# Attention with relative bias, then a maxout feed-forward: the order of VectorE's work in batch one's second pass, and of batch four's DMA transposes

## The chip, the cores and the metric

The kernel runs on one core of a Trainium2 chip. A core has five engines, each with its own instruction stream: TensorE (PE, with its weight loads listed apart as PEld), VectorE (DVE), ScalarE (ACT), GpSimd (POOL) and SyncE (SP). They run side by side and meet at semaphores. DMAs are issued by an engine's stream and carried out by 16 DMA engines. The metric is the time of one execution on the device, in microseconds (us), less is better.

## The reference

Attention over 8 batches and 8 heads of 576 tokens with 64 numbers each, with a bias that depends on the distance of two tokens only; its output, turned to one row of 512 per token, goes through a feed-forward with three gates of which the largest is kept.

```python
scores = scale * np.matmul(q, k.transpose(0, 1, 3, 2))
bias = bias_table[bucket]                       # bucket of |i - j|
scores = scores + bias.transpose(2, 0, 1)[None, :, :, :]
attn = np.exp(scores - max); attn = attn / (sum + 1e-09)
x = np.matmul(attn, v)                          # to (4608, 512)
h = np.maximum(np.maximum(x @ w1, x @ w2), x @ w3)
return (h @ w_out)
```

## The kernel before

**Tiling.** The heads are worked on in pairs (`hp` 0 to 3), the tokens in four tiles of 128 and a rest of 64. `b` counts the batches from 0: batch one is `b = 0`, batch four is `b = 3`. Queries and keys stand turned, with the head's numbers along the partitions, in `qT` and `kT` (two buffers each, one for every other batch).

**A pair's work.** `visit` makes the scores of one half of the queries on TensorE (tiles `sc`) and their exponentials on ScalarE (into `e4`). The rest of 64 keys goes through `left_keys` (scores `sct`), the rest of 64 queries through `left_queries` (scores `scq`), both into `el`. The bias is a factor after the exponential. It differs from a constant only near the diagonal, so VectorE multiplies bands alone: `times_band` takes one key tile's band in `e4` with `hank`, a table of the factors in SBUF; `times_bandt` and `times_band_left` (together `products`) do the same for `el`, the first with `bandt`, a mirrored copy of a part of `hank` that `make_bandt` makes once with two copies. `attend` then makes the weighted sums of one half (`half` 0 or 1) in PSUM tile `a` and returns `quotients`, the division on VectorE (a reciprocal, L730, and a multiplication, L731, into `x_sb`).

**Batch one** is done in two passes, since its data come in late. The first pass makes the scores of the first half of the queries for all four pairs; each pair's `attend` of half 0 is put on the list `late`. The second pass makes the second half and takes one or two entries from `late` for every pair (`next_late`). In pair 0 and 1 it runs two of them, with `bands(2)` and `bands(3)`, the first pass's bands of pairs 2 and 3, between them. `late_bands` are the three bands of the second pass of the pair itself. In the midst of each pair's `visit`, `more_transposes(hp + 1)` turns the next pair's remaining queries on TensorE, and a VectorE copy (L110, `qT<-tp`, 128x320) brings them to `qT`. `x_transposes` turns the finished output into `xT` on TensorE, and ScalarE copies it. Here and later `fill` puts in portions of the feed-forward.

**Order.** Matmuls, VectorE's and ScalarE's operations run in the order of the program (`inorder`); exponentials are free in this stage. So what stands ahead of an operation in the program on the same engine must be over before it starts.

**Batches two to eight.** Batch two's queries and keys are turned on TensorE. From batch three on, `transposes(b)` lets SP issue DMA transposes from `q_sb`, `k_sb` and the tails into `qT` and `kT`: it is a generator, and every `next(crossbar)` issues the q and the k transpose of one tile (`t` 0 to 3, then the tail as `t` 4), L550. SP also issues the stores of finished output rows (`store_outputs`, which issues what has been put on `stores`) and the transposes of `x_sb` into `xT` (L741). In the loop over `b` and `hp` there are two places for `next(crossbar)` per pair: behind the first `visit`, and behind the second half of the scores. For `b` 2 the first place issues in pairs 1 to 3, the second in pairs 1 and 2, each behind a call of `store_outputs`.

**Loads tied to transposes.** GpSimd's queue issues the loads of q, k and v. `go_behind` makes a load wait for a transpose: `load_v(b + 1)` in pair 2 of `b` 2 waits for `turned_qk[3, 1, 2]`, the key transpose of tile 2 of batch four, and `load_qk(b + 2)`, the loads of batch five, for that of tile 3. TensorE needs tile 2 and 3 of the keys in the second `scores` of pair 0, and the tail of the keys in `left_keys`.

Of the kernel before, what the change touches and what calls it, by code (L numbers as in the profile page):

```python
# [39 lines left out]
def kernel(  # L40
# [68 lines left out]
    def dve_copy(out_, in_):  # L109
        return inorder(nc.vector.tensor_copy(out_, in_))  # L110
# [199 lines left out]
    def make_bandt():  # L310
        for par in range(2):
            r = slice(64 * par, 64 * par + 64)
            c = BAND // 2 - 64 * par
            dve_copy(bandt[r, :, :], hank[r, par::2, c : c + 192][:, :, ::-1])
# [337 lines left out]
    def visit(qT, kT, e4, c, mid=None, el=None):  # L652

        if el is not None:
            banks = [ps_a.tile([P, KT * 64], F32, tag="a", name="scq") for _ in range(2)]
            turn_left_queries(qT, kT, banks)
            put_left_queries(el, banks)
        for tt in range(0, KT, 2):
            scores(qT, kT, e4, c, tt)
            if tt == 0 and mid:  # L660
                mid()
# [12 lines left out]
    def times_bandt(hp, el):  # L674
        return inorder(nc.vector.tensor_tensor(
            out=el[:, S - 192 : S], in0=el[:, S - 192 : S], in1=bandt[:, hp, :], op=ALU.mult
        ))
# [8 lines left out]
    def times_band_left(hp, el):  # L686
        last_tile = el[:, S + P * KT - P :].rearrange("p (h q) -> p h q", h=2)
        inorder(nc.vector.tensor_tensor(
            out=last_tile, in0=last_tile, in1=hank[:, 2 * hp : 2 * hp + 2, P - 64 : P][:, :, ::-1], op=ALU.mult,
        ))  # L690
# [69 lines left out]
    def next_late():  # L760
        return late.pop(0)() if late else (lambda: None)

    def e_tiles():
        return (
            ep.tile([P, KT, 2, QM], BF16, tag="e4", name="e4"),
            ep.tile([P, S + KT * P], BF16, tag="el", name="el"),
        )
# [37 lines left out]
    def bands(hp):  # L805
        for t in range(KT):
            times_band(hp, first_e[hp], t, 0, QS, inorder)
# [9 lines left out]
    for hp in range(HP):  # L817
        qT, kT = (x[:, hp, :] for x in qk[0])
        e4, el = e_tiles()
# [22 lines left out]
    def products(hp, el):  # L842
        times_bandt(hp, el)
        times_band_left(hp, el)

    for hp in range(HP):
        qT, kT = (x[:, hp, :] for x in qk[0])
        e4, el = e_tiles()  # L850
        visit(qT, kT, e4, 1, (lambda: more_transposes(hp + 1)) if hp + 1 < HP else None)

        def keys():
            left_keys(hp, qT, kT, el, QS, S)

        def queries():
            left_queries(hp, qT, kT, el)

        def late_bands():
            for t in range(KT):  # L860
                times_band(hp, e4, t, QS, QM, inorder)

        if hp == 0:
            keys()
        if hp == 1:
            x_transposes(0, 0)
        quotients = next_late()
        if hp < 2:
            quotients()
            if hp == 0:  # L870
                bands(2)
            else:
                keys()
            queries()
            if hp == 1:
                x_transposes(1, 0)
            quotients = next_late()
            quotients()
            if hp == 0:
                bands(3)  # L880
                make_bandt()
            late_bands()
            products(hp, el)
        else:
            keys()
            quotients()
            queries()
            late_bands()
            if hp == 2:
                x_transposes(2, 0)  # L890
                x_transposes(3, 0)
                add_ffn(0, QS)
                fill(8)
            else:
                batch[2] = load_tiles()
                load_qk(2)
                x_transposes(0, 1)
                fill(8, lambda: second_transposes(qk[1], 0))
            products(hp, el)
        late.append(lambda hp=hp, e4=e4, el=el: attend(0, hp, e4, el, 1))  # L900

    turned = [lambda hp=hp: x_transposes(hp, 1) for hp in range(1, HP)]
    for b, hp in [(b, hp) for b in range(1, B) for hp in range(HP)]:
        if hp == 0:
            x_sb[b] = x_tile()
        qT, kT = (x[:, hp, :] for x in qk[b])
        e4, el = e_tiles()
        together = b > 1 and (b, hp) != (2, 0)
        tiled = bool(stages)
        rate = 8 if b == 1 or (b, hp) == (2, 0) else 13  # L910

        visit(qT, kT, e4, 0)
        store_outputs()
        if b == 1:
            if hp == 0:
                crossbar = transposes(2)
            next(crossbar, None)
        elif hp and b + 1 < B:  # L920
            if hp == 1:
                crossbar = transposes(b + 1)
            next(crossbar)
        early()
        if turned:
            turned.pop(0)()
        quotients = next_late()
        if not tiled:
            times_band(hp, e4, 0, 0, QS, inorder)
        quotients()  # L930
        if b == 1 and hp + 1 < HP:
            spread_packed(hp + 1, nc.vector)
        if (b, hp) == (1, 1):
            add_ffn(QS, QS)

        def keys():
            sums_first = together and (not tiled or len(pending) < 2)
            if sums_first:
                next_late()()
            left_keys(hp, qT, kT, el, 0, S)  # L940
            if together and not sums_first:
                next_late()()

        if tiled:
            if len(pending) > 1:
                fill(DCH)
            keys()
            fill(FCH)
            times_band(hp, e4, 0, 0, QS, inorder)
            begin0, end0, begin1, end1, after = stages.pop(0)  # L950
            scores(qT, kT, e4, 1, 0)
            begin0()
            exp_left = left_queries(hp, qT, kT, el)
            turned_1 = begin1()
            times_band(hp, e4, 1, 0, QM, inorder)
            band_left = times_bandt(hp, el)
            go_behind([band_left], turned_1[-1])
            times_band_left(hp, el)
            scores(qT, kT, e4, 1, 2)
            dve0 = end0([exp_left])  # L960
            dve1 = end1([band_left])
            times_band(hp, e4, 2, 0, QM, inorder)
            dve0()
            times_band(hp, e4, 3, 0, QM, inorder)
            dve1()
            pending.extend((n, [fn]) for n, fn in after)
        else:
            fill(8 if (b, hp) == (2, 1) else rate, keys, *([lambda: None] if together else []))
            times_bandt(hp, el)
            visit(qT, kT, e4, 1, el=el if together else None)  # L970
        store_outputs()
        if b == 1 or hp in (1, 2) and b + 1 < B:
            next(crossbar, None)
        early()
        if turned:
            turned.pop(0)()
        if not together:
            quotients = next_late()
            times_band(hp, e4, 1, 0, QM, inorder)
            quotients()  # L980
        if b == 1 and hp + 1 < HP:
            second_transposes(qk[1], hp + 1)
        if hp == 1 and b > 1:
            pending.extend((n, [fn]) for n, fn in rest)
            rest.clear()
            made, tail = ffn((b - 1) * CH, CH, False, True)
        if hp == (2, 2, 0)[min(b, 3) - 1] and b + 1 < B:
            load_v(b + 1, 0, H, turned_qk[b + 1, 1, b] if b < 3 else None)
            if b == 1:
                load_last_weights(turned_qk[2, 1, KT - 1])  # L990
                batch[3] = load_tiles()
                load_qk(3, turned_qk[2, 1, KT - 1])
        if hp == 2 and 1 < b < B - 2:
            batch[b + 2] = load_tiles()
            load_qk(b + 2, turned_qk[b + 1, 1, KT - 1])

        def queries():
            if not together:
                left_queries(hp, qT, kT, el)
            times_band(hp, e4, 3, 0, QM, inorder)  # L1000

        def bands_2():
            for t in range(1 if together else 2, 3):
                times_band(hp, e4, t, 0, QM, inorder)

        if not tiled:
            fill(rate, bands_2, queries)
            times_band_left(hp, el)
        if hp == 1 and b > 1:
            stages.extend(made)  # L1010
            strict.append(b)
        for half in range(2):
            late.append(lambda b=b, hp=hp, e4=e4, el=el, half=half: attend(b, hp, e4, el, half))
# [48 lines left out]
```

## Time and profile before

The median of 5 runs is 315.74 us (315.17 to 316.11).

| What | us |
|---|---|
| profiled execution | 315.74 |
| its span | 314.0 |
| PE busy | 300.7 |
| ACT busy | 205.2 |
| DVE busy | 213.6 |
| POOL busy | 110.6 |
| PE busy from 18.00 to 24.00 (6.00) | 4.89 |
| PE busy from 24.00 to 30.00 (6.00) | 5.17 |
| PE busy from 66.00 to 95.00 (29.00) | 27.95 |
| PE busy from 95.00 to 127.00 (32.00) | 31.79 |

The span runs from the first instruction of the program to the last; the execution's own time holds what lies around it too. Busy times of the engines overlap. In the lines of a timeline the columns are the start and the time taken in us, the engine, the line of the program, the operation, what it writes and reads, the shape, and how many are merged into the line; in brackets stands the idle time of the engine before it and what ended that. The second pass of batch one runs from about 15 to 32 us, `b` 2 from about 68 to 90, and batch four begins at about 90.

### The profile page before, as it was taken

To read this page: it belongs to the slowest core of one execution; us is meant where nothing else is said; L and a number is where in the kernel's file an instruction comes from. 1 tells how busy PE (TensorE), PEld (TensorE's weight loads), DVE (VectorE), ACT (ScalarE), POOL (GpSimd) and SP (SyncE) were. 2 spreads that over 40 slices of the span, in tenths; PEclk is the share of its full clock that TensorE was granted. 3 is DMA by queue.
4 is the path that set the end of the run, shared out by engine and by line. 5 is a ranking of instruction groups with operands and counts; after the bars stand their busy time and mean duration, and the time that the engine had idled before them with its cause. 6 is when DMAs were issued, how large, how long until landed. Compare 5 with 4: busy or idle time off the path is not lost.

```text
span 314.0 us, 9008 instructions
## 1 busy us (share of the span) xinstructions
PE 300.7 (96%) x3721; PEld 177.5 (57%) x3750; DVE 213.6 (68%) x535; ACT 205.2 (65%) x280; POOL 110.6 (35%) x147
## 2 busy tenths in 40 slices
PE   7877999999999999999999999999999999999995
PEld 2355777775554655565556655665556554444442
DVE  6488778776776767776777677767776775553552
ACT  3997888897776677777777777777777741122221
POOL 8968651781069521950195029500000000000000
PEclk9999999999999999999999999999999999999999
DMA  9999999999999999999899969994322103302103
GB/s 164 194 189 200 182 157 114 138 156 129 187 189 137 158 207 138 129 121 204 147 117 157 200 127 142 139 194 104 61 44 101 38 17 75 121 0 94 42 0 134
DMA packets 163945, 40.39 MB, mean 129 GB/s; under 512 B 153784, under 2 KB 159424, under 8 KB 163904
## 3 DMA queue, kind: packets, MB, share of 16 engines
q0 software_dynamic: 103840, 16.66, 82.0%
q1 hardware_dynamic: 58304, 22.69, 41.5%
q10 hardware_dynamic: 1760, 0.47, 0.7%
q8 instruction: 29, 0.48, 0.6%
q14 instruction: 12, 0.10, 0.1%
HBM read 35.39 MB, written 9.45 MB: 143 GB/s over the span
## 4 chain that ended last, share of the span: by engine, by line
PE 84%; ACT 7%; DMA 2%; DVE 2%; SPq 2%; issue 2%; DVEq 0%; ACTq 0%
PE ps L94 25%; PE psp L410 23%; PE a L94 14%; PE sc L94 9%; PE pso L94 8%; ACT e L625 6%; PE sct L94 2%; PE scq L94 2%; DMA kT<-ktail 2%; SPq L550 1%; PE warm L94 1%; PE tp L97 1%; ACT el L625 1%; DMA out_dram<-osb 1%; DVE e L619 1%
## 5 line engine op out<-in xcount | busy, mean ns | idle before, releaser
L625 ACT ACTIVATE e<-sc 128x1024 bf16<-128x1024 f32 x128 | 126.6, 1026 | 32.5 <-PE sc L94 29.6
L94 PE MATMUL ps<-xT,w_bf 128*128 128x512 bf16 (+1 forms) x427 | 89.3, 343 | 1.2
L619 DVE TENSOR_TENSOR e<-e,hank 128x512 bf16<-128x512 bf16 (+2 forms) x136 | 61.5, 466 | 31.9 <-ACT e L625 31.7
L410 PE MATMUL psp<-xT,w_bf 64*128 64x512 bf16 x544 | 66.2, 376 | 0.0
L94 PEld LDWEIGHTS <-w_bf 128*128 128x128 bf16 x448 | 40.4, 98 | 32.3 <-issue 0.5
L94 PEld LDWEIGHTS <-kT 64*128 64x128 bf16 (+1 forms) x832 | 33.6, 95 | 37.9 <-issue 16.3
L94 PE MATMUL sc<-qT,kT 64*128 64x256 bf16 x512 | 44.8, 274 | 3.0 <-ACT e L625 0.9
L94 PE MATMUL a<-vx,e 128*128 128x65 bf16 x1024 | 44.3, 193 | 0.0
L94 PEld LDWEIGHTS <-e 128*128 128x128 bf16 x1024 | 40.4, 97 | 2.0
L362 DVE TENSOR_TENSOR hT<-ps,m 128x512 bf16<-128x512 f32 x48 | 33.2, 691 | 7.7 <-PE ps L94 6.1
L410 PEld LDWEIGHTS <-w_bf 64*128 64x128 bf16 x544 | 25.3, 94 | 20.9
L167 POOL DMA_DIRECT2D q_sb<-in_q_dram x24 | 22.0, 916 | 41.2 <-DMA kT<-k_sb 28.5
L94 PE MATMUL a<-vt,el 128*128 128x130 bf16 x160 | 35.6, 223 | 0.0
L139 POOL DMA_DIRECT2D vx<-in_v_dram x28 | 24.8, 909 | 26.4 <-PE psp L410 15.3
L731 DVE TENSOR_TENSOR x_sb<-a,rd 128x256 bf16<-128x256 f32 (+1 forms) x64 | 31.4, 491 | 2.2
L625 ACT ACTIVATE el<-sct 128x576 bf16<-128x576 f32 (+2 forms) x36 | 21.8, 607 | 13.4 <-PE sct L94 12.6
L347 ACT ACTIVATE m<-ps 128x512 bf16<-128x512 f32 x14 | 8.4, 597 | 33.4 <-PE ps L94 33.4
L94 PEld LDWEIGHTS <-el 128*128 128x128 bf16 x416 | 24.0, 97 | 9.9 <-issue 7.0
L94 PE MATMUL pso<-wo_bf,hT 128*128 128x512 bf16 (+2 forms) x124 | 28.4, 369 | 0.4
L434 DVE TENSOR_TENSOR m<-psp,m 128x512 bf16<-128x512 f32 x34 | 23.4, 687 | 0.0
L167 POOL DMA_DIRECT2D k_sb<-in_k_dram x24 | 22.0, 916 | 3.5 <-DMA w_bf<-in_moe_w_dram 2.3
L107 ACT ACTIVATE m<-psp 128x512 bf16<-128x512 f32 x34 | 20.2, 595 | 3.6 <-PE psp L410 3.6
(80 smaller groups left out, 272.9 us busy)
## 6 DMA issues: line engine op xcount, KB each, us to landing
out_dram<-osb SPq DMA_DIRECT2D x35, 256.0 KB, 3.8
vx<-in_v_dram POOLq DMA_DIRECT2D x28, 128.0 KB, 8.1
q_sb<-in_q_dram POOLq DMA_DIRECT2D x26, 128.0 KB, 6.5
k_sb<-in_k_dram POOLq DMA_DIRECT2D x24, 128.0 KB, 7.6
w_bf<-in_moe_w_dram POOLq DMA_DIRECT2D x3, 768.0 KB, 10.4
xT<-in_k_dram SPq DMA_DIRECT2D x6, 128.0 KB, 4.9
hank<-w_dr SPq DMA_DIRECT2D x2, 384.0 KB, 5.1
wo_bf<-in_moe_w_out_dram POOLq DMA_DIRECT2D x1, 768.0 KB, 7.9
```

Source lines behind the costliest of these rows:

```text
L94: inorder(nc.tensor.matmul(*args, **kw))
L97: inorder(nc.tensor.transpose(*args))
L107: return inorder(nc.scalar.activation(out=out_, in_=in_, func=ACTF.Copy))
L139: in_turn(b, nc.gpsimd.dma_start(out=dst[:, t, h0:h1, :], in_=x[:, t, h0:h1, :])) for t in range(t0, t1)
L167: loads.append(in_turn(b, nc.gpsimd.dma_start(out=dst[:, t], in_=main_part(src, b)[:, t])))
L347: nc.scalar.activation(out=st[fb]["m0"][:], in_=ps0, func=ACTF.Copy)
L362: inorder(nc.vector.tensor_tensor(out=block(fb), in0=ps2, in1=other, op=ALU.max))
L410: made.append(inorder(nc.tensor.matmul(ps[i][:, 0:w], lhsT=lhsT, rhs=rhs, start=not swap and c == 0, stop=swap and c == n - 1,)))
L434: inorder(nc.vector.tensor_tensor(out=m[:], in0=ps[1][:], in1=m0[:], op=ALU.max))
L619: put(nc.vector.tensor_tensor(out=e4[:, t, :, lo:hi], in0=e4[:, t, :, lo:hi], in1=hank[:, 2 * hp : 2 * hp + 2, c0:c1][:, :, ::-1], op=ALU. ...
L625: made = nc.scalar.activation(out=out_, in_=in_, func=ACTF.Exp, scale=inv_sqrt_d)
L731: divided[b, hp, half] = inorder(nc.vector.tensor_tensor(out=x_sb[b][:, 2 * half : 2 * half + n, P * hp : P * hp + P].rearrange("p t (h d) ...
```

## The change

In batch one's second pass, `make_bandt` moves from behind `bands(3)` to the front of pair 0's quotients. The late bands and products of pairs 0 and 1 are no longer made at the end of their own pair; they are put on a list, `behind`, and made in the next pair: pair 0's behind the first quotients of pair 1, pair 1's ahead of `keys` and the quotients of pair 2. In `b` 2, pair 1, the first place issues two tiles of transposes in place of one, so that tiles 2, 3 and 4 come one place sooner each; the first place of pair 3 finds none left. Nothing is computed that was not computed before, and nothing is left out.

```diff
@@ -845,6 +845,7 @@
+    behind = []
     for hp in range(HP):
         qT, kT = (x[:, hp, :] for x in qk[0])
         e4, el = e_tiles()
@@ -856,7 +857,7 @@
         def queries():
             left_queries(hp, qT, kT, el)
 
-        def late_bands():
+        def late_bands(hp=hp, e4=e4):
             for t in range(KT):
                 times_band(hp, e4, t, QS, QM, inorder)
 
@@ -866,10 +867,13 @@
             x_transposes(0, 0)
         quotients = next_late()
         if hp < 2:
+            if hp == 0:
+                make_bandt()
             quotients()
             if hp == 0:
                 bands(2)
             else:
+                behind.pop()()
                 keys()
             queries()
             if hp == 1:
@@ -878,10 +882,10 @@
             quotients()
             if hp == 0:
                 bands(3)
-                make_bandt()
-            late_bands()
-            products(hp, el)
+            behind.append(lambda late_bands=late_bands, hp=hp, el=el: (late_bands(), products(hp, el)))
         else:
+            if behind:
+                behind.pop()()
             keys()
             quotients()
             queries()
@@ -920,7 +924,9 @@
         elif hp and b + 1 < B:
             if hp == 1:
                 crossbar = transposes(b + 1)
-            next(crossbar)
+            next(crossbar, None)
+            if (b, hp) == (2, 1):
+                next(crossbar)
         early()
         if turned:
             turned.pop(0)()
```

## The prediction

> **What bounds the kernel now.** I read the busy table first, then the chain of waits for the two places that the change touches, then the timelines of the engines there, and last the issue times and landings of the DMAs.
>
> ```profile
> PE 300.7 (96%) x3721; PEld 177.5 (57%) x3750; DVE 213.6 (68%) x535; ACT 205.2 (65%) x280; POOL 110.6 (35%) x147
> ```
>
> TensorE is busy 300.7 of 314.0 us, so a change that takes no matmul away can win at most the 13.3 us that are left, and only where TensorE, or an engine that it follows, stands still. The second pass of batch one is such a place. First TensorE, then ScalarE, then VectorE:
>
> ```profile
> 24.07 0.39 PE L94 MATMUL sc<-qT,kT 64*128 64x256 bf16 x4 [0.68 <-DVE qT L110]
> 24.50 1.94 ACT L625 ACTIVATE e<-sc 128x1024 bf16<-128x1024 f32 x2 [0.93 <-PE sc L94]
> 17.37 0.32 DVE L110 COPY qT<-tp 128x320 bf16<-128x320 bf16 x1
> 18.91 0.18 DVE L730 RECIPROCAL rd<-a 128x4 f32<-128x4 f32 x1 [1.23 <-PE a L94]
> ...
> 21.77 0.72 DVE L110 COPY bandt<-hank 64x768 bf16<-64x768 bf16 x2
> 22.51 0.96 DVE L619 TENSOR_TENSOR e<-e,hank 128x256 bf16<-128x256 bf16 x3
> 23.39 0.25 DVE L675 TENSOR_TENSOR el<-el,bandt 128x192 bf16<-128x192 bf16 x1
> 23.56 0.21 DVE L688 TENSOR_TENSOR el<-el,hank 128x128 bf16<-128x128 bf16 x1
> 23.70 0.31 DVE L110 COPY qT<-tp 128x320 bf16<-128x320 bf16 x1
> ```
>
> The scores of pair two wait 0.68 us for a copy of turned queries (start 23.70), and ScalarE stands 0.93 us behind them. The copy could have run from 21.77, but behind it in VectorE's order lie bandt, the late bands and the two products of pair zero. At 18.91 VectorE had been idle for 1.23 us.
>
> The other place is the start of batch four, where TensorE waits twice for transposes that SP issues:
>
> ```profile
> 91.60 0.28 PE L94 MATMUL sc<-qT,kT 64*128 64x256 bf16 x2 [0.23 <-DMA kT<-k_sb]
> 94.95 0.42 PE L94 MATMUL sct<-qT,kT 128*128 128x512 bf16 x2 [0.61 <-DMA kT<-ktail]
> 73.56 2.60 SPq L550 DMA_TRANSPOSE kT<-k_sb  x1
> 79.58 1.01 SPq L391 DMA_DIRECT2D out_dram<-osb  x2
> 80.68 2.89 SPq L550 DMA_TRANSPOSE qT<-q_sb  x1
> 90.17 1.21 SPq L550 DMA_TRANSPOSE kT<-ktail  x1
> ```
>
> That is 0.23 + 0.61 = 0.84 us. SP's timeline has no hole over 0.1 us from 72.20 to 91.38: SP is full there, and the last issue is late because of all that is issued ahead of it.
>
> **The change, part by part.** *make_bandt* (two copies, 0.72 us together) moves to 17.69, where the copy that starts at 17.37 ends. It reads the whole of hank; the bands at 16.83 read it already, and its two loads were issued from 10.91 to 11.83, 5.1 us from landing in the median, so it is there. 17.69 + 0.72 = 18.41, 0.50 ahead of the quotients at 18.91: hidden by that idle time. Without the cover it would cost up to 0.72, by delaying the quotients, bands(2) and what follows.
>
> *The late bands and products of pair zero* (0.88 + 0.31 us by their starts, 22.51 to 23.70) go behind the copy and the first quotients of pair one's stage, those of pair one behind the next copy. The copy then starts at 21.77 in place of 23.70, 1.93 us sooner. TensorE's work before the scores ended at 24.07 - 0.68 = 23.39, so 0.68 of the 1.93 counts; ScalarE, free at 23.57, starts its exponentials at 24.50 - 0.68 = 23.82. What is late next? After the copy VectorE does quotients (0.63), late bands and products (1.19): done at 22.08 + 1.82 = 23.9. The weighted sums that read them start on TensorE at 24.99 - 0.68 = 24.3, a margin of 0.4. The next copy of queries, at 27.03 before, comes by about 24.6 and has 28.77 - 0.68 to be ready. Pair one's two products, 0.67 and 0.62 us beside two GpSimd copies (25.70 to 27.03) against 0.25 and 0.21 elsewhere, still meet those copies; VectorE has over a microsecond in hand. **Term one: -0.68** (from -0.93, ScalarE's whole idle time, to 0).
>
> *From there to batch four.* Loads on GpSimd's queue do not follow the compute, they follow each other: the third gate weight is issued at 32.55 and lands 10.4 us later, at 42.95. Its first matmul runs at 43.55, so that a shift of 0.68 would put it at 42.87; with some 0.05 us from landing to start it waits till 43.0. **Term two: +0.15**, from 0 to 0.3. All else of batch two and three that I checked has over 0.5 us left, except batch two's transposed output, read by the first matmuls at 78.96, which SP issues from 64.63 on; these issues are released by VectorE and shift with it. A shift of 0.53 reaches batch four.
>
> *The transposes on SP.* The order was t0, store, t1, two stores, t2, store, t3, t4 (each t a q and a k transpose); it becomes t0, t1, store, t2, two stores, t3, store, t4. So t1 passes one store (0.53 us), t2 three less one, t3 one; **t4 passes none**, and t4 is what the longer wait is for. Nothing on SP waits in this stretch, so t4's issue moves only as SP's start moves (its issue at 67.98 follows VectorE's quotients, so by up to 0.53) and as the long issues fall: ten transposes took 14.8 us in batch three (43.99 to 58.77), and here 19.2 less 2.1 for four stores = 17.1, because three of them lasted 2.60, 2.89 and 1.85 instead of 1.2. Why, no row says. The trace doesn't bound how they fall in a new order. If t4 is issued 0.84 sooner relative to TensorE, both waits vanish (-0.84); if its landing stays where it is, the whole shift is eaten (+0.53). I take **term three: -0.3**, from the 17.1 that is 2.3 above batch three's 14.8: one long issue less of the three would already be enough, and I give that a bit over a third.
>
> The move also starts other DMAs: batch four's v loads (6 on GpSimd's queue, 89.30 to 94.07) are tied to the landing of t2's keys, the q and k loads of batch five, behind them, to t3's. Both start one to two microseconds sooner, and run beside the last transposes. What this costs is bounded by latencies from issue to landing: 4.7 for the last transpose now, 4.6 and 5.1 for the two key transposes before it, 8.6 for the key transpose at 73.56, issued while loads were under way. The last one already runs with the v loads in flight (issued at 90.17, v from 89.30), so I take its own row, 4.7, and no added cost; 8.6 stands for the upper end.
>
> The Trainium skill, page "DMA: Bandwidth & Descriptors", section "Queues, rings and completion order", says that every DMA engine takes turns between the queues that have work, packet by packet, so that no queue goes first. That speaks against the change: by it the last transposes lose half their engines to loads that used to start later, and by the doubled latency (an estimate from that page, 4.7 more) the kernel would come out about 4 us slower. The 4.7 of the last transpose, taken with loads in flight, doesn't show a half lost, and I go by the row.
>
> **Sum.** -0.68 + 0.15 - 0.30 = -0.83. The profiled execution took 315.74 us (span 314.0, 1.74 around it), which is also the median of the runs, so 314.9 us. From batch four on, TensorE runs close to full (31.79 of 32.00 us from 95 to 127) and keeps what it has won. This case's own range: 314.2 (-0.68 - 0.84) to 315.1.
>
> **The rivals.**
> *The DMA takes it back.* The landings at batch four do not move: loads, not compute, pace SP's queue (the last key load of batch four, issued at 68.91, took 15.6 us to land). Then the wait of 0.84 grows by 0.53 and the end stands: 315.7, between 315.5 and 316.0. For it: DMA engines at nine tenths in every slice up to there, t4 passes nothing. Against it: between 86 and 91 us the transposes landed 4.6 to 5.1 after issue, which is an issue-bound queue.
>
> *The loads crowd out t4 (slower).* Place: 86 to 97 us, the last key transpose. Price: its latency in place of 4.73. It decides from 4.73 + 0.53 + 0.63 = 5.9 us on. The nearest row of transposes among v loads are batch five's four key transposes (4.5, median 6.2, 8.3): at the median +1.5 - 0.53 = +0.9, so 316.7; at 8.6, +3.3, 319.1. For it: the v loads come one to two microseconds sooner. Against it: six loads are of the same size as before, and t4's own latency had them in flight.
>
> *The second pass gains nothing*, because the weighted sums at 24.3 wait for the products moved behind: a margin of 0.4 us. Price: the 0.68, so with term three alone 315.4; it counts with the first rival.
>
> **How the numbers follow.** Forecast 0.58; DMA takes it back, or nothing gained in the second pass, 0.24; loads crowd t4 out, 0.18. 0.2% of 315.74 is 0.63 us, about what a measurement of this kernel can tell from no change. The forecast lies 0.83 below, so its chance goes to faster: faster 0.58, same 0.24, slower 0.18. The range goes from 314.1, both waits gone, up into the slower case, 316.4, which leaves out most of that one and little else.
>
> **What would show it.** Step one: two bandt copies before the first quotients, no 0.68 wait before pair two's scores, exponentials at about 23.8. Step two: the third weight's first matmul at about 43.0 and a shift of 0.5 at 60 us. Step three: SP's order as above; the sum of the waits for kT at batch four's first pair under 0.84, and v loads from about 87.5. Wrong would be: a wait for kT of over 1.3 us there (the DMA took it back), a last key transpose that lands over 5.9 us after issue (crowded out), or a new VectorE wait at 24.3.

## The result and the profile after

| | before | after |
|---|---|---|
| median of all runs, us | 316.36 (80 runs, 314.60 to 320.73) | 316.90 (43 runs, 314.44 to 319.27) |
| ratio after to before, 95% interval | 1 | 1.0014 (0.9998 to 1.0029) |
| profiled execution, us | 315.74 | 316.38 |
| its span, us | 314.0 | 314.6 |

The change can't be told from none: the interval takes in 1, and nearly all of it lies on the slower side. The prediction was 314.9, faster. The median of before over all its runs is 0.6 us above that of the first five; between groups of runs it went from 315.97 to 316.37, so kernels are compared below by ratios to before's runs on the same chip. The ratios leave out the few runs that took over 1.5% more than the fastest of their kernel, and they are not the quotients of the medians beside them. "Faster" and "slower" below mean that the interval of the ratio does not reach 1; all these differences are half a percent or less.

**The second pass** does what was foreseen. VectorE's timeline of after (start, time taken, engine, line, operation):

```profile
18.64 0.78 DVE L110 COPY bandt<-hank 64x768 bf16<-64x768 bf16 x2
19.95 0.18 DVE L730 RECIPROCAL rd<-a 128x4 f32<-128x4 f32 x1 [0.53 <-PE a L94]
...
22.79 0.32 DVE L110 COPY qT<-tp 128x320 bf16<-128x320 bf16 x1
23.03 0.17 DVE L730 RECIPROCAL rd<-a 128x4 f32<-128x4 f32 x1
23.23 0.42 DVE L731 TENSOR_TENSOR x_sb<-a,rd 128x256 bf16<-128x256 f32 x1
23.57 0.95 DVE L619 TENSOR_TENSOR e<-e,hank 128x256 bf16<-128x256 bf16 x3
24.44 0.25 DVE L675 TENSOR_TENSOR el<-el,bandt 128x192 bf16<-128x192 bf16 x1
24.61 0.21 DVE L688 TENSOR_TENSOR el<-el,hank 128x128 bf16<-128x128 bf16 x1
```

Of VectorE's idle time ahead of the quotients 0.53 us is left (it was 1.23): the two bandt copies stand in what was idle. The copy of turned queries stands ahead of the late bands. TensorE's timeline and then ScalarE's, both of after, at the scores of pair two:

```profile
24.32 0.39 PE L94 MATMUL sc<-qT,kT 64*128 64x256 bf16 x4
```

```profile
24.76 1.94 ACT L625 ACTIVATE e<-sc 128x1024 bf16<-128x1024 f32 x2
```

There is no bracket on either line: the waits of 0.68 and 0.93 are gone. Both start later than before all the same, because this execution came to the second pass later. The mark for that is the last scores of the first pass, just ahead of it (the expectations below call them the second pass's first scores, which start 1.19 us later in both). First before, then after:

```profile
14.68 0.39 PE L94 MATMUL sc<-qT,kT 64*128 64x256 bf16 x4 [0.47 <-ACT e L625]
```

```profile
15.72 0.39 PE L94 MATMUL sc<-qT,kT 64*128 64x256 bf16 x4 [0.27 <-ACT e L625]
```

From there to pair two's scores it is 24.32 - 15.72 = 8.60 us in place of 24.07 - 14.68 = 9.39, so the second pass won **0.79 us**. The later beginning is no work of the change, as the table of all profiles below shows.

**Batch four** takes it back. TensorE's timeline of after:

```profile
95.60 0.42 PE L94 MATMUL sct<-qT,kT 128*128 128x512 bf16 x2 [1.47 <-DMA kT<-ktail]
```

The wait for tile 3 of the keys (0.23) is gone, that for the tail went from 0.61 to 1.47. SP's timeline of after, then GpSimd's:

```profile
83.96 1.22 SPq L550 DMA_TRANSPOSE qT<-q_sb  x1
85.27 1.22 SPq L550 DMA_TRANSPOSE kT<-k_sb  x1
86.58 1.82 SPq L391 DMA_DIRECT2D out_dram<-osb  x1
88.50 1.22 SPq L550 DMA_TRANSPOSE qT<-qtail  x1
89.82 1.28 SPq L550 DMA_TRANSPOSE kT<-ktail  x1
```

```profile
85.20 3.52 POOL L139 DMA_DIRECT2D vx<-in_v_dram  x4 [14.91 <-PE ps L94]
88.69 1.28 POOL L158 DMA_DIRECT2D vt<-in_v_dram  x2
```

The order is the new one, a store between tile 3 and the tail. The last key transpose is issued at 89.82 (before 90.17), but takes 5.73 us to land where it took 4.73, and lands at 95.55 in place of 94.90. The v loads now start 4.62 us ahead of that issue, at 85.20; before it was 0.87. GpSimd's timeline of before, then a line of its chain of waits:

```profile
89.30 3.52 POOL L139 DMA_DIRECT2D vx<-in_v_dram  x4 [14.30 <-PE psp L410]
```

```profile
90.17 4.73 DMA kT<-ktail
```

The chain of waits of after, around that place (start, time, what):

```profile
87.15 0.69 DVE hT L362
87.84 0.34 DVE e L619
88.18 0.22 SPq L391
...
88.50 1.22 SPq L550
...
89.82 5.73 DMA kT<-ktail
95.55 0.05 issue
95.60 0.42 PE sct L94 x2
```

The chain goes through the landing, and ahead of it through the store, which is put down to a product of VectorE that ended at 88.18. That part is doubtful: VectorE's last copy of output rows ahead of this store started at 79.03 and took 0.69 us, so the rows were there long before, and in the two later profiles of after the same store took 0.53 us, not 1.82. Before, no store stood between tile 3 and the tail. Busy times by stage, after (stretch and its length, then busy time and instructions of PE, PEld, DVE, ACT, POOL):

```profile
66.00:95.00 29.00, 27.91 (x407) 17.20 (x409) 21.68 (x54) 21.62 (x28) 11.06 (x14) 1.00 1.91 162
95.00:127.00 32.00, 31.20 (x426) 18.30 (x431) 21.68 (x53) 23.49 (x31) 14.41 (x19) 1.00 1.60 153
```

TensorE has lost 0.59 us in the second stretch (31.20 against 31.79 before), about what the longer wait takes of it (95.60 - 95.00 = 0.60). Set side by side, the same matmuls of TensorE run 1.04 us later in after just ahead of the second pass, 0.25 later at pair two's scores, 0.21 sooner at the first scores with tile 3 of batch four's keys (91.39 against 91.60), and 0.65 later from the left-over keys (95.60 against 94.95) to the last matmul (310.75 against 310.10). The 0.65 is 95.55 - 94.90, the difference of the landings. In this pair of profiles, what TensorE had won or lost ahead of that wait counts for nothing.

### The profile page after: what moved, and what is told of

It reads as the page before. It is cut to its first block, busy times and chain, and to the rows that moved or that the text cites. A ratio compares the mean times of both kernels' runs of the same rounds, so it can differ in the third digit from the quotient of the medians.

```text
span 314.6 us, 9005 instructions
## 1 busy us (share of the span) xinstructions
PE 301.5 (96%) x3721; PEld 177.8 (57%) x3750; DVE 213.2 (68%) x535; ACT 205.4 (65%) x280; POOL 110.8 (35%) x147
## 3 DMA queue, kind: packets, MB, share of 16 engines
q0 software_dynamic: 103840, 16.66, 79.8%
## 4 chain that ended last, share of the span: by engine, by line
PE 83%; ACT 6%; DMA 6%; issue 2%; DVE 1%; SPq 0%; POOL 0%; POOLq 0%; DVEq 0%; ACTq 0%
PE ps L94 24%; PE psp L410 23%; PE a L94 13%; PE sc L94 9%; PE pso L94 8%; ACT e L625 5%; DMA qT<-q_sb 3%; PE sct L94 2%; DMA kT<-ktail 2%; PE scq L94 2%; DMA out_dram<-osb 1%; PE tp L97 1%; ACT el L625 1%; SPq L550 0%; ACT xT L107 0%
```

## The experiments

**Theory.** The landing of batch four's last key transpose sets the start of the left-over keys' scores. What TensorE wins ahead of it becomes a longer wait; and that landing comes late when the v loads have started well ahead of the transpose's issue. **Rivals.** The new order on SP alone is at fault (later issues, stores between); the second pass gives nothing, and a later beginning of it belongs to the change; or the time is lost behind batch four.

**One part at a time.** First the changed kernel with SP's order as before, so that only the second pass differs:

```diff
-            next(crossbar, None)
-            if (b, hp) == (2, 1):
-                next(crossbar)
+            next(crossbar)
```

> Part one alone: bandt and the late bands moved, SP's order as before. Differences are of the same matmul's start, against the profile of before, less the difference at the second pass's first scores (14.68 us before), so that the start-up drops out. Theory A (the second pass wins, batch four takes back through the last transposes): -0.7 to -0.8 us from pair two's scores (24.07 before) on; at batch four the two waits for kT, 0.84 us before, grow by what of the shift the transposes do not follow, to 0.9 to 1.6; end -0.1 to -0.8. Theory B (the whole is a gain and the timed difference is noise of the start-up): -0.7 to -0.8 kept to the end. Theory C (the moved bands cost something at the start): a start-up that is 0.5 to 1 us later again, as in the profile of the changed kernel (1.04 later at the second pass's first scores).

Measured: 315.72 us, 0.9998 (0.9983 to 1.0014). The second pass won its time here too (8.62 us to pair two's scores), and this execution even came to the second pass 0.57 us sooner than before's, so that pair two's scores ran 1.34 us ahead of before's. TensorE's timeline of this kernel at batch four:

```profile
94.63 0.42 PE L94 MATMUL sct<-qT,kT 128*128 128x512 bf16 x2 [2.10 <-DMA kT<-ktail]
```

The wait is 2.10 us, and the last matmul starts at 310.10, as before. So the second pass alone gives nothing that the timing can tell, without any new order on SP. The other part alone is the kernel before with the three lines of the new order put in:

> Part two alone: the transposes of batch four issued sooner, VectorE's order as before. Theory A: no difference up to batch four; batch four's v loads start 3 to 4 us sooner, the wait for tile 3's keys goes (-0.23), the last key transpose takes 5.5 us or more from issue to landing in place of 4.73 and the waits together come to 1.0 to 1.5, so the end is +0.2 to +0.7 later. Theory B: the waits together are 0.84 or less, the end 0 to -0.3. Theory C: start-up as in before.

Measured: 317.00 us, 1.0048 (1.0014 to 1.0082), slower. The last key transpose in this kernel's trace (its issue, who waited, and the time to landing):

```profile
L550 SPq DMA_TRANSPOSE kT<-ktail x1: 1747/1747/1747, 88.7 to 88.7; - x1
...
  PE sct L94: 0.7, 1
...
DMA to landing us min/median/max: 7.2/7.2/7.2
```

It is issued 1.4 us sooner than before and lands 1.07 later, at 95.97; the v loads had started at 84.69. The wait is short, 0.7 us, since TensorE itself was late: this execution came to the second pass at 16.09. Here an earlier issue of the tail was no gain, as the loads had started sooner by more.

**The v loads held back.** In the changed kernel, they wait for the key transpose of tile 3 in place of tile 2:

```diff
-            load_v(b + 1, 0, H, turned_qk[b + 1, 1, b] if b < 3 else None)
+            load_v(b + 1, 0, H, turned_qk[b + 1, 1, b + (b == 2)] if b < 3 else None)
```

> The changed kernel, but batch four's v loads wait for the key transpose of tile 3 instead of tile 2 (one DMA later). Theory A (the sooner v loads crowd the last transposes): v loads start near 91 us, the last key transpose takes under 5 us again, the waits for kT together are under 0.9, and the end is 0.3 to 0.8 us ahead of the changed kernel's, start-up taken out (-0.7 to -1.2 against before). Theory B (crowding is not the cause, SP's queue is): latency and wait as in the changed kernel, 5.7 and 1.2.

Measured: 315.06 us, 0.9962 (0.9939 to 0.9984), faster. The last key transpose of this kernel, then TensorE's timeline:

```profile
L550 SPq DMA_TRANSPOSE kT<-ktail x1: 1206/1206/1206, 88.0 to 88.0; - x1
...
DMA to landing us min/median/max: 2.5/2.5/2.5
```

```profile
92.40 0.41 PE L94 MATMUL sct<-qT,kT 128*128 128x512 bf16 x2
99.51 0.22 PE L94 MATMUL a<-vt,el 128*128 128x130 bf16 x1 [1.29 <-DMA vt<-in_v_dram]
```

Issued 0.85 us ahead of the first v load, the transpose lands after 2.46 us, and the wait is gone. The price stands in the last line: v's tail, issued last of the six loads, lands at 99.38, and the weighted sums wait 1.29 us for it. On top of that edit, tile 3's transposes issued in pair 1's second place behind tile 2's, and so the tail's one place sooner, in pair 2's first:

```diff
             next(crossbar, None)
+            if (b, hp) == (2, 1):
+                next(crossbar)
```

> As e3, and one tile more is issued in the second place of pair one of the third batch: tiles 2 and 3 ahead of two stores, the tail ahead of the last store. The tail so passes a store, which in the changed kernel it does not. Theory A and the SP queue alike: the last key transpose is issued 0.5 to 2 us sooner (88 to 89.3 us), lands before TensorE wants it, no wait for kT of over 0.2 us, end -1.2 to -1.6 against before with the start-up taken out. If the DMA engines pace it (their loads, not the issue): it lands no sooner than 94 us and the wait stays over 0.6.

Measured: 315.82 us, 0.9997 (0.9967 to 1.0026). The v loads wait for tile 3 as in the kernel above, and the tail's latency is 3.87 us with no wait. But in the profiled execution, one of this kernel's slowest at 317.94, TensorE lost the time one batch later:

```profile
127.09 0.28 PE L94 MATMUL sc<-qT,kT 64*128 64x256 bf16 x2 [3.33 <-DMA kT<-k_sb]
```

This is a wait of 3.33 us for batch five's keys, whose transposes are issued from 102 to 123 us among batch five's v loads. How often it comes is not known from one profile; by the ratio this order gives nothing that can be told from before. Then the kernel before with the v loads behind tile 3, and nothing else changed:

> The kernel before, with one edit: batch four's v loads wait for the key transpose of tile 3 instead of tile 2. Theory A (the time from issue to landing of the last key transpose follows from how far ahead of it the v loads start): v loads start at or behind that transpose's issue, it lands 2.4 to 4 us after issue (4.73 before), the waits for kT fall from 0.84 to under 0.3, the weighted sums that read batch four's v wait up to 1.5 us for it instead, ratio 0.996 to 1.002. Theory B (SP's issue order sets the landing): latency 4.7 as before and the same 0.84.

Measured: 316.14 us, 1.0013 (0.9982 to 1.0045). The latency is 2.46 us again and the wait for the tail gone, but the weighted sums wait 0.6 us for v's tail. Holding back v alone trades one wait of before for another.

**Looked at again.** One more profile each of before and after showed how much of the above is scatter.

> The kernel before once more, for its profile: how much the start-up (second pass's first scores at 14.68 us), the v loads' lead over the last key transpose (0.87), its time to landing (4.73) and the waits for kT (0.84) move from one execution to another. Start-up within 1 us, the wait between 0.3 and 1.5, if it is noise.

Measured: 316.42 us. Here the kernel before has its v loads at 86.23, 3.27 us ahead of the last key transpose, which then took 6.06 us, not 4.73. GpSimd's timeline of this profile, then the transpose:

```profile
86.23 3.53 POOL L139 DMA_DIRECT2D vx<-in_v_dram  x4 [15.80 <-PE ps L94]
```

```profile
L550 SPq DMA_TRANSPOSE kT<-ktail x1: 1241/1241/1241, 89.5 to 89.5; - x1
...
DMA to landing us min/median/max: 6.1/6.1/6.1
```

So the row that the prediction went by was one draw.

> The changed kernel once more, for its profile. If the start-up was chance, the second pass's first scores are not always a microsecond late (15.72 in its first profile); 0.78 won at pair two's scores again; v loads 3 to 5 us ahead of the last key transpose, 5.5 us or more from its issue to landing, 1 to 2 us of waits for kT.

Measured: 317.19 us. Latency 5.91, landing at 96.31, waits of 0.9 us for tile 3 and 1.4 for the tail.

**Two of the six v loads early, four late.** The first two stay behind tile 2, the other four wait for tile 3, in the changed kernel:

```diff
-    def load_v(b, h0, h1, behind=None):
-        loads = load_main(v, b, h0, h1, vx[b % 2][:, :, :, 0:D])
-        go_behind(loads + load_tail(v, b, h0, h1, v_diag), behind)
+    def load_v(b, h0, h1, behind=None, then=None):
+        loads = load_main(v, b, h0, h1, vx[b % 2][:, :, :, 0:D]) + load_tail(v, b, h0, h1, v_diag)
+        go_behind(loads[:2], behind)
+        go_behind(loads[2:], then or behind)
...
-            load_v(b + 1, 0, H, turned_qk[b + 1, 1, b] if b < 3 else None)
+            load_v(b + 1, 0, H, turned_qk[b + 1, 1, b] if b < 3 else None, turned_qk[3, 1, 3] if b == 2 else None)
```

> The changed kernel, but of batch four's six v loads two go behind the key transpose of tile 2 (as in the change) and four behind that of tile 3. Theory A: the last key transpose takes 3 to 4.5 us, lands before or within 0.3 us of TensorE's need, v is there 1.5 to 2 us sooner than in the run with all v loads behind tile 3 (99.4) and nothing waits for it; ratio 0.993 to 0.997, the best of all. Theory B: latency 5.7 as in the changed kernel, ratio 1.000 to 1.003.

Measured: 315.24 us, 0.9958 (0.9931 to 0.9984), faster than before and than the change. GpSimd's timeline of this kernel, then TensorE's:

```profile
86.41 1.77 POOL L139 DMA_DIRECT2D vx<-in_v_dram  x2 [13.71 <-PE sct L94]
90.27 1.75 POOL L139 DMA_DIRECT2D vx<-in_v_dram  x2 [2.09 <-PE psp L411]
92.01 1.26 POOL L158 DMA_DIRECT2D vt<-in_v_dram  x2
```

```profile
93.86 0.41 PE L94 MATMUL sct<-qT,kT 128*128 128x512 bf16 x2
```

The transpose is issued at 89.82, as in after, but in the pause between the loads, and lands after 3.60 us in place of 5.73; v's tail is there at 96.11. Nothing waits, and TensorE is busy in both stretches throughout:

```profile
66.00:95.00 29.00, 29.00 (x415) 17.49 (x413) 21.59 (x54) 22.17 (x29) 9.81 (x13) 1.00 1.73 167
95.00:127.00 32.00, 32.00 (x457) 19.19 (x457) 23.17 (x56) 23.88 (x31) 15.11 (x20) 1.00 1.67 152
```

The last matmul starts at 309.01. On another chip, side by side: this kernel again; the same with SP's order as before; the same with the second pass as before; and the change as it was.

> The changed kernel with the split v loads, once more, beside the two runs that leave one part out and the changed kernel itself: ratio 0.993 to 0.998 again, no wait for kT over 0.3 us.

> Part one (the moved bands) and the split v loads (two behind tile 2, four behind tile 3), SP's order as before: the changed kernel's part two left out. If the sooner issue of the transposes is worth nothing by itself once the loads are split, this equals the run with both (ratio 0.994 to 0.998, no wait for kT over 0.3 us). If passing one store matters, tile 3's keys or the tail's come 0.3 to 0.8 us later and a wait for kT of that size is back, ratio 0.997 to 1.000.

> Part two with the split v loads, without part one: the second pass as in before. If the second pass's gain of 0.78 us reaches the end once nothing waits at batch four, this is about 0.8 us (0.25%) behind the run with both, ratio 0.996 to 1.000 with no wait for kT over 0.3 us; pair two's scores 9.4 us behind the second pass's first scores, not 8.6. If the loads pace batch four, it is as fast as the run with both.

> The changed kernel, timed on the same chip as the three others: ratio 1.000 to 1.003, v loads 3 to 5 us ahead of the last key transpose, its latency 5.5 us or more, waits for kT of 1 to 2.5 us together at batch four's first pair.

Measured, beside 316.37 us for before on that chip:

| v loads | second pass | SP's order | us | ratio, 95% interval |
|---|---|---|---|---|
| split | new | new | 315.47 | 0.9950 (0.9925 to 0.9975) |
| split | new | old | 315.54 | 0.9961 (0.9935 to 0.9988) |
| split | old | new | 316.40 | 0.9975 (0.9954 to 0.9997) |
| as they were | new | new | 317.75 | 1.0026 (0.9995 to 1.0056) |

The split is worth 0.0076 of the time in the changed kernel (1.0026 against 0.9950, intervals apart). With it, the second pass is worth 0.0025 (0.9975 against 0.9950), which is 0.79 us of 316.37, just what it wins; but these intervals overlap, so it is a reading and not proof, the more so as the third row's median is no better than before's. What SP's order adds once the loads are split is not settled (0.9950 against 0.9961): in the one profile with the old order the v loads start only at 88.35, the transpose takes 5.00 us and a wait of 1.1 us is back, where at most 0.3 was expected, while its median lies by the first row's. The kernel before with the split alone was not run.

**All profiles together.** "2nd pass" is the start of the last scores of the first pass, just ahead of the second, "to pair two" the time from there to pair two's scores; "v" the first v load of batch four, "lead" how far it is ahead of the issue of the last key transpose; "wait" TensorE's for that transpose; "end" the start of the last matmul. All in us.

| kernel | 2nd pass | to pair two | v | lead | latency | lands | wait | end | end - lands |
|---|---|---|---|---|---|---|---|---|---|
| before | 14.68 | 9.39 | 89.30 | 0.87 | 4.73 | 94.90 | 0.6 | 310.10 | 215.20 |
| before, again | 15.50 | 9.39 | 86.23 | 3.27 | 6.06 | 95.56 | 0.9 | 310.77 | 215.21 |
| after | 15.72 | 8.60 | 85.20 | 4.62 | 5.73 | 95.55 | 1.5 | 310.75 | 215.20 |
| after, again | 15.54 | 8.61 | 86.37 | 4.03 | 5.91 | 96.31 | 1.4 | 311.53 | 215.22 |
| after, third (clock 0.987) | 14.84 | 8.61 | 85.68 | 2.80 | 6.74 | 95.22 | 2.0 | 312.05 | 216.83 |
| second pass only | 14.11 | 8.62 | 86.40 | 2.34 | 5.85 | 94.59 | 2.1 | 310.10 | 215.51 |
| SP's order only | 16.09 | 9.46 | 84.69 | 4.04 | 7.24 | 95.97 | 0.7 | 311.25 | 215.28 |
| v behind tile 3 | 14.14 | 8.61 | 88.86 | -0.85 | 2.46 | 90.47 | 0 | 309.44 | - |
| and tail sooner | 15.36 | 8.61 | 89.06 | 0.09 | 3.87 | 93.02 | 0 | 312.32 | - |
| before, v behind tile 3 | 15.05 | 9.57 | 90.17 | -1.02 | 2.46 | 91.61 | 0 | 310.42 | - |
| v split | 15.62 | 8.61 | 86.41 | 3.41 | 3.60 | 93.42 | 0 | 309.01 | - |
| v split, other chip | 14.41 | 8.62 | 86.72 | 2.29 | 4.08 | 93.09 | 0.3 | 308.64 | 215.55 |
| v split, second pass only | 15.40 | 8.61 | 88.35 | 1.57 | 5.00 | 94.92 | 1.1 | 310.12 | 215.20 |
| v split, SP's order only | 14.74 | 9.60 | 86.70 | 3.42 | 3.86 | 93.98 | 0 | 309.22 | - |

Three things are read from it. The time to pair two falls into two groups, 9.39 to 9.60 with the old second pass and 8.60 to 8.62 with the new one: that part holds in every profile. The start lies between 14.1 and 16.1 with either, so the later beginning of after's first profile is scatter. And wherever TensorE waited for the last key transpose, the end follows its landing by 215.2 us, in five profiles to within 0.02; 215.28 is close to them, and of the other three one had a lower clock and two another wait behind this one (0.3 us in batch five, and 0.5 us of weight loads for v's tail). The latency is 2.46 where the v loads began after the issue, 3.6 to 5.0 where they had a pause or had just begun, and 5.7 to 7.2 where they had run without a pause for over two microseconds.

The runs do not part the v loads from what follows them. Batch five's q and k loads stand behind them on GpSimd's queue, and whatever holds v back holds these back too. In the six profiles with 5.7 us or more the first of them is issued over three microseconds ahead of the transpose's landing (91.51 against 95.55 in after), in all others at most 0.9 ahead. So the loads of that queue delay the transpose; what share is v's own is open.

## Why the prediction was wrong

**Term one, the second pass (-0.68): right.** It won 0.79, the bandt copies took 0.78 us in VectorE's idle time, and the products moved behind were in time: the rival that the second pass gains nothing falls.

**Term two, the third gate weight (+0.15): not there.** In after it was issued at 31.8 and landed 9.3 us later, at 41.1, where before it had taken 10.4, and the matmuls from there on show no wait for it. Nor is there one in the kernel with the second pass alone, where the first of them starts at 42.15, 1.40 sooner than before. It was right to ask what is late next, but this was not it.

**Term three, the transposes on SP (-0.3): the step that failed.** The prediction saw that the v loads would start sooner beside the last transposes, and then wrote "so I take its own row, 4.7, and no added cost". The measured latency in three profiles of after is 5.73, 5.91 and 6.74 us. In the first pair of profiles the tail was issued 0.35 us sooner (89.82 against 90.17), about the size of term three, but its latency grew by 1.00 (5.73 against 4.73): it landed 0.65 later. Two things were wrong with the row. It was taken as a transpose's latency with the loads in full flight, but they had begun 0.87 us ahead of it; in a second profile of the same kernel they led by 3.27, and it took 6.06. And it was taken to hold no loss from sharing, since no row told what the transpose takes alone. Where the loads begin only after its issue it is 2.46 us, and by that 4.73 already held a loss of 2.27.

The rule that was weighed and set aside, in the Trainium skill, page "DMA: Bandwidth & Descriptors", section "Queues, rings and completion order", that DMA engines take turns between queues with work, pointed the right way. Its estimate of 4.7 us more on top of 4.73 was too much; set on the 2.46, a doubling would be 4.9 (an estimate from that page). The runs show 3.6 to 7.2 where loads had begun ahead of it, so that a doubling is not the upper end.

The v loads were foreseen "from about 87.5" and came at 85.20. "t4 passes none" was right: the tail gained only those 0.35 us. In after the store that now stands between tile 3 and the tail took part of the gain; at a usual 0.53 us it would have ended 1.29 us sooner (86.58 + 0.53 = 87.11 against 88.40). Whether SP waited there is not shown, so "Nothing on SP waits in this stretch" is open for the new order.

**The rivals.** "The DMA takes it back" is what happened. Its sign, a wait for kT of over 1.3 us, is there at 1.47, and the kernel with the second pass alone shows it by itself: TensorE 1.34 us ahead, the wait at 2.10, the end where it was. Its price, nothing won, was too kind by the later landing in the first pair of profiles; over all runs it fits, the interval taking in 1. "The loads crowd out t4" was to decide from 5.9 us of latency on; 5.73, 5.91 and 6.74 lie around that, and SP's order alone is indeed slower, at 1.0048. The two are one mechanism and were priced as two; together they had 0.42 against the forecast's 0.58. The sentence that TensorE "keeps what it has won" from batch four on was right where no other wait followed, as the constant 215.2 shows. But what is won ahead of a landing is not yet won.

## What to carry to other kernels

Time won ahead of a wait for a transfer is kept only if the transfer, too, comes sooner; so find the landing behind the place that is mended, and ask whether it follows the compute or other transfers. A latency read from one profile belongs to the traffic of that moment: look at when its neighbours were issued, and take a second profile before leaning on it. If a small transfer that sets the pace runs beside large ones with time in hand, leave a pause for it: here two of six loads early and four late made 1.0026 into 0.9950.

## What the runs showed of the hardware

The same key transpose of the tail landed 2.46 us after its issue in both kernels where the v loads began after it, and up to 7.24 us after where they had begun some four microseconds ahead of it.

The transposes' issues on SP take 1.2 us each, but in the profiles of before and after two to five of the ten in this stretch take 1.4 to 2.9, at other places from run to run. In both profiles of the first comparison a 16 KB load on the queue of instructions often falls in with them. From after's page (queue, packets, MB, share) and from SP's timeline of after:

```profile
q8 instruction: 29, 0.48, 0.7%
```

```profile
73.95 1.89 SPq L550 DMA_TRANSPOSE kT<-k_sb  x1
75.93 1.30 SPq L550 DMA_TRANSPOSE qT<-q_sb  x1
77.32 1.83 SPq L550 DMA_TRANSPOSE kT<-k_sb  x1
79.25 0.53 SPq L391 DMA_DIRECT2D out_dram<-osb  x1
79.87 1.59 SPq L550 DMA_TRANSPOSE qT<-q_sb  x1
```

After's instruction loads in this stretch run at 73.5 and 79.8, beside the first and the last of the three long issues; the one at 77.32 has none. Before, they run at 73.8, 81.4 and 87.9, beside issues of 2.60, 2.89 and 1.85 us. Another of after's, at 86.5, falls on the store of 1.82 us, which the chain puts down to VectorE instead. In before's second profile they run at 74.1, 79.8 and 86.9, beside an issue of 2.15, a store of 0.76 and an issue of 2.14 us. That is a coincidence in time and was not tried by itself; nor is it known why one execution comes to the second pass at 14.1 us and another at 16.1.
